# The last sums of y of the first pair of batches by accumulating GpSimd transfers, and other weights of two engines in the planner

## The chip, the cores and the metric

The kernel runs on one core of a Trainium2 chip. The metric is the device time of one execution in microseconds (us). The kernel before took 1038.81 us in the median of three runs (1038.71 to 1040.23).

The engines of the core are named as the profile names them: PE multiplies matrices (PEld loads its weights), DVE is VectorE, ACT is ScalarE, POOL is GpSimd, and SP only issues transfers (SPq is its queue). Each engine works through its own instructions strictly in order, so an instruction that waits holds up everything behind it on that engine.

## The reference

The input is four batches of attention with twelve heads, followed by two feed-forward blocks. Without the set-up it reads:

```python
# q, k, v: (4, 12, 448, 64)
scores = cap * tanh(q @ k.T / 8 / cap)          # cap = 30
attn = softmax(scores); x = attn @ v            # laid out as (1792, 768)
h = x @ w_in                                    # 768 -> 2048
g = h * cos(h)
y = g @ w_out                                   # 2048 -> 768
a = y @ w1; b = y @ w2                          # 768 -> 1024 each
out = (a * b @ w3) @ w_out2                     # 1024 -> 1024 -> 768
```

All inputs are 32-bit floats for the first part, and the weights come as 64-bit floats, which the kernel turns into 32-bit floats itself.

## The kernel before, in words

**Arithmetic.** A product of two 32-bit matrices is made of three passes on PE (lines 390, 391, 392): high half by high half, weight high by data low, weight low by data high. So each operand first has to be split into a high part (a cast, line 366 on ACT, 367 on DVE, 370 on POOL) and a low part (a subtraction, line 376 on DVE, 378 on POOL). Names that end in h and l are these parts (xh, xl, wih, wil, woh, wol). The 64-bit weights are converted by a scaling (lines 925 and 926), a masked copy (line 931, on POOL or, by the same line's other option, line 933 on DVE) and two bit operations on DVE (938 and 942).

**Stages.** Attention of all heads comes first, with the products of w3 and w_out2 (they don't depend on the data) mixed in. From about 160 us on, the first feed-forward block of the first pair of batches (b = 0 and 1) runs beside the attention of the second pair. Its work is cut into units: unit u is one group of 256 of the 2048 inner columns for one batch, and units of b = 0 and b = 1 take turns. A unit makes h with PE, its gate on ACT and DVE (the tile g with a high and a low part), and then y_part (line 1126 and on) multiplies g by two slices of w_out into six banks of PSUM, one for each m from 0 to 5. Each y_part is six passes of 448 columns, three for each of the unit's two blocks of 128 inner columns. The first group's y is copied into the tile y; every later group's is added to it (TENSOR_TENSOR y<-bank,y). After the last unit of a batch SP writes the six slices of y to DRAM (y_d). The second pair of batches uses seven products instead of eight in a two-by-two scheme of blocks (h_step); for it x_lefts loads the stored x, makes sums and differences of the blocks and splits them all, and h_rights does so for the weights. A product of this kind has three steps k, each of three passes. While h_step of the first pair of columns runs, PE also does the twelve y_parts of the last two units of b = 0 and 1. Later early_lefts loads y_d of b = 0 and 1 and prepares the second block, which fills the rest of the time.

**What sets the order.** Nothing is issued in the order of the source. Each piece of work is given to a planner (class Plan) with a due time, a list of engines that could do it with the planner's cost on each, and what it reads and writes. schedule goes through time, takes the ready pieces by due time, and gives each to the engine with the smallest sum of its waiting time and its cost. The cost is multiplied by a weight wACT, wDVE or wPOOL while the due time is below tw; before, all three weights were 1. A helper named port tells which pieces need the port that DVE and POOL share; by it every piece on POOL does. The planner's result is one fixed list of instructions for each engine. The same file holds a second, general program for large values of cap, which isn't executed with cap = 30.

Of the kernel before, what the change touches and what calls it, by code (L numbers as in the profile page):

```python
# [15 lines left out]
ALU = mybir.AluOpType  # L16
# [4 lines left out]
B, H, S, D = 4, 12, 448, 64  # L21
# [10 lines left out]
BH = B // 2  # L32
# [105 lines left out]
class Plan:  # L138
# [57 lines left out]
    def schedule(self):  # L196
# [10 lines left out]
        free = dict(PE=1.0, ACT=2.0, DVE=3.4, POOL=1.5, SP=1.2, port=0.0)  # L207

        def port(x):
            return x[0] == "POOL" or len(x) > 3  # L210

        free[None] = 0.0
        table, order, t, line = "exp", [], 0.0, 0.0
# [94 lines left out]
    wlead=3.1,  # L308


    wACT=1.0, wDVE=1.0, wPOOL=1.0, tw=396.0, back=1.13,
    nq=1, nqh=2, nph=2, npl=2,
    nraw=3, nx=2, w3bufs=2, w2bufs=6,
)
# [1 line left out]
    tw=432.21,  # L316
# [24 lines left out]
def program(  # L341
# [12 lines left out]
    general=False,  # L354
):
    nc = tc.nc
    PE, ACT, DVE, POOL, SP = nc.tensor, nc.scalar, nc.vector, nc.gpsimd, nc.sync
    G = dict(PAR, **GENERAL) if general else PAR
    plan = Plan()
# [4 lines left out]
    def copy(due, dst, src, n, on, psum=False):  # L364
        opts = {
            "A": ("ACT", (0.051 if psum else 0.094) + n / 1200, lambda: ACT.copy(dst(), src())),  # L366
            "D": ("DVE", 0.068 + n / (960 if psum else 1920), lambda: DVE.tensor_copy(dst(), src()))  # L367
            + (() if psum else (True,)),
            "P": ("POOL", 0.16 + n / 1200,
                  lambda: POOL.tensor_scalar(dst(), src(), 1.0, 0.0, op0=ALU.mult, op1=ALU.add)),  # L370
        }
        plan.op(due, [opts[e] for e in on], r=[src], w=[dst])
# [12 lines left out]
    def dma(due, dst, src, r=(), w=(), kb=115, write=False):  # L385
        plan.op(due, [("SP", 0.66, lambda: SP.dma_start(dst(), src()))], r=r, w=w,
                kb=kb)

    def mm3(out, wh, wl, xh, xl, first, last, on=False):
        PE.matmul(out, wh, xh, start=first, stop=False, skip_group_check=on)  # L390
        PE.matmul(out, wh, xl, start=False, stop=False, skip_group_check=on)  # L391
        PE.matmul(out, wl, xh, start=False, stop=last, skip_group_check=on)  # L392
# [60 lines left out]
    psum = pools["psum"].pool  # L453
# [24 lines left out]
    y_d = Scratch("dram", [B, KD, P, S], "y_d")  # L478
# [538 lines left out]
    def pair_due(n):  # L1017
        d = G["pd"]
        return unit_due(2 * NP) + (n - 0.26 * (n > 1)) * d
# [36 lines left out]
    def moe1(raw_r, x_r):  # L1056
# [14 lines left out]
        of = {b: [u for u, x in enumerate(units) if x[1] == b] for b in range(B)}  # L1071
# [58 lines left out]
        def y_part(u, m, due):  # L1130
            g, b = units[u]
            gh, gl = g_t[u]
            if u == of[b][0] and m == 0:
                yacc[b] = y_r.new()
            acc = hy_r.ref()
            ws = [w_t["o", g, c] for c in range(2)]

            def f():
                for c in range(2):
                    mm3(acc()[:, :S], ws[c][0]()[:, m * P:(m + 1) * P], ws[c][1]()[:, m * P:(m + 1) * P],  # L1140
                        gh()[:, c, :], gl()[:, c, :], c == 0, c == 1)

            plan.op(due, [("PE", 6 * MM, f)], r=[gh, gl, *ws[0], *ws[1]], w=[acc])
            ya = yacc[b].at(m, lambda t: t[:, m, :])
            if u == of[b][0]:
                copy(due + 1, ya, acc[:, :S], S, "AD", psum=True)
            else:
                tt(due + 1, ya, acc[:, :S], ya, S, ALU.add, psum=True)
            if u == of[b][-1]:
                z = y_d.at((b, m), lambda d: d[b, m])  # L1150
                dma(due + 3, z, ya, r=[ya], w=[z], kb=230, write=True)

# [137 lines left out]
        for u, (g, b) in enumerate(units[:2 * NP]):  # L1290
# [4 lines left out]
            for c in range(2):  # L1295
                wi = w_t["i", g, c]
                hp = hy_r.ref()
                for kp in range(3):
                    due = u0 + (c * 3 + kp) * pu / 6
# [3 lines left out]
                            r=[*wi, *(z.at(k) for k in ks for z in (xh[b], xl[b]))], w=[hp])  # L1303
# [14 lines left out]
        for n in range(NP):  # L1318
            u, u0, u1 = 2 * NP + 2 * n, pair_due(n), pair_due(n + 1)
# [415 lines left out]
```

## Time and profile before

| | |
|---|---|
| median of 3 runs | 1038.81 us |
| the profiled execution | 1039.48 us |
| its span (first to last instruction) | 1037.7 us |
| PE busy | 1012.4 us (98% of the span) |
| DVE busy | 934.6 us (90%) |
| ACT busy | 576.2 us (56%) |
| POOL busy | 254.8 us (25%) |
| transfers | 174.36 MB, mean 168 GB/s |

How to read it: 1.78 us of the profiled execution lie outside its span. Busy time is a union over the instructions of an engine; on PE and DVE an instruction starts before the one ahead has ended, so the sum of durations is larger than the busy time. The granted clock of PE was full for the whole span but for one short stretch near 495 us and the time after the last matmul.

### The profile page before, as it was taken

What the parts mean: (1) busy time and instruction counts of PE and PEld (TensorE: products, weight loads), DVE (VectorE), ACT (ScalarE), POOL (GpSimd) and SP (SyncE); (2) the same over time, 40 slices, a digit from 0 to 9 for tenths busy, and PEclk for the clock granted to TensorE, in tenths of its full rate; (3) what the DMA queues carried; (4) which work ended last, traced back from release to release, by engine and by line L of the source; (5) the groups of instructions that cost most, each with busy time, mean ns of one, the idle gap of its engine ahead of it and who ended that gap; (6) DMA issues with size and microseconds to landing.
All of it is one profiled execution on the core that took longest, in us unless ns stands there. A gap on an engine that the chain in (4) does not pass through costs nothing.

```text
span 1037.7 us, 15441 instructions
## 1 busy us (share of the span) xinstructions
PE 1012.4 (98%) x5524; PEld 864.6 (83%) x5524; DVE 934.6 (90%) x1418; ACT 576.2 (56%) x799; POOL 254.8 (25%) x203
## 2 busy tenths in 40 slices
PE   7999999989999999999999999999999999999997
PEld 2577777757788887798899999999898999999996
DVE  5999999999999999999999889999899889777982
ACT  6778787888777777725464433543334346222440
POOL 3453220222344321225303223211122100111110
PEclk9999999999999999999999999999999999999999
DMA  8776896867665655653545321319455556433442
GB/s 273 199 199 188 224 252 175 229 186 206 210 178 189 195 155 165 190 173 112 203 130 180 109 62 46 122 49 302 146 195 185 166 154 228 149 123 121 138 134 83
DMA packets 86648, 174.36 MB, mean 168 GB/s; under 512 B 19874, under 2 KB 59682, under 8 KB 86562
## 3 DMA queue, kind: packets, MB, share of 16 engines
q1 hardware_dynamic: 86562, 173.28, 54.4%
q8 instruction: 45, 0.74, 0.3%
q14 instruction: 41, 0.34, 0.1%
HBM read 131.30 MB, written 41.77 MB: 167 GB/s over the span
## 4 chain that ended last, share of the span: by engine, by line
PE 78%; DVE 11%; DMA 5%; issue 3%; ACT 1%; POOL 1%; SPq 1%; DVEq 0%; POOLq 0%; ACTq 0%
PE bank L390 23%; PE bank L392 23%; PE bank L391 22%; PE bank L702 4%; PE double L659 2%; PE double L658 2%; PE bank L707 1%; DMA rawc<-in_w_out 1%; DMA rawc<-in_w_in 1%; DMA kr<-in_k 1%; DVE stl L938 1%; DVE p L376 1%; DVE xl L376 1%; PE double L648 1%; DMA rs<-zs 1%
## 5 line engine op out<-in xcount | busy, mean ns | idle before, releaser
L390 PE MATMUL bank<-g,woh 128*128 128x448 f32 x384 | 140.6, 366 | 3.8 <-DVE zs L367 2.8
L392 PE MATMUL bank<-g,wol 128*128 128x448 f32 x384 | 139.1, 362 | 0.0
L391 PE MATMUL bank<-g,woh 128*128 128x448 f32 x384 | 138.8, 361 | 0.0
L673 ACT ACTIVATE double<-double,ts 112x896 f32<-112x896 f32 x96 | 93.8, 982 | 29.9 <-PE double L659 22.6
L376 DVE TENSOR_TENSOR y<-bank,y 128x448 f32<-128x448 f32 x168 | 101.5, 616 | 9.1 <-PE bank L392 8.8
L673 ACT ACTIVATE p<-double,pac 112x896 f32<-112x896 f32 x96 | 96.5, 1014 | 3.1 <-PE bank L707 1.8
L366 ACT COPY hs<-bank 128x448 f32<-128x448 f32 x74 | 39.4, 532 | 105.7 <-PE bank L392 105.6
L390 PE MATMUL bank<-xh,wih 128*128 128x448 f32 x264 | 96.6, 366 | 1.3 <-ACT xh L366 1.3
L391 PE MATMUL bank<-xl,wih 128*128 128x448 f32 x264 | 96.0, 364 | 1.2 <-POOL xl L378 1.2
L392 PE MATMUL bank<-xh,wil 128*128 128x448 f32 x264 | 96.5, 366 | 0.7 <-POOL wil L378 0.7
L390 PEld LDWEIGHTS bank<-g,woh 128*128 128x128 f32 x384 | 72.2, 188 | 15.2 <-DVE zs L367 3.2
L702 PE MATMUL bank<-p,v 112*32 112x448 f32 x768 | 77.6, 542 | 1.0 <-ACT w L1102 1.0
L392 PEld LDWEIGHTS bank<-g,wol 128*128 128x128 f32 x384 | 72.2, 188 | 5.2
L391 PEld LDWEIGHTS bank<-g,woh 128*128 128x128 f32 x384 | 72.1, 188 | 4.8
L931 POOL TENSOR_SCALAR wx<-rawc 128x768 f32<-128x768 f32 x29 | 39.8, 1371 | 94.7 <-ACT rawc L925 72.6
L376 DVE TENSOR_TENSOR p<-p 112x448 f32<-112x448 f32 x79 | 58.3, 738 | 2.4 <-ACT p L673 2.0
L702 PEld LDWEIGHTS bank<-p,v 112*32 112x32 f32 x768 | 22.3, 109 | 45.0 <-issue 41.0
L658 PE MATMUL double<-qh,ks 128*112 128x448 f32 x160 | 58.7, 367 | 0.0
L659 PE MATMUL double<-ql,ks 128*112 128x448 f32 x160 | 58.3, 365 | 0.0
L390 PEld LDWEIGHTS bank<-xh,wih 128*128 128x128 f32 x264 | 49.8, 189 | 8.3 <-issue 2.9
L391 PEld LDWEIGHTS bank<-xl,wih 128*128 128x128 f32 x264 | 49.8, 189 | 5.0 <-POOL xl L378 1.5
L392 PEld LDWEIGHTS bank<-xh,wil 128*128 128x128 f32 x264 | 49.9, 189 | 4.5 <-POOL wil L378 1.1
(356 smaller groups left out, 2786.0 us busy)
## 6 DMA issues: line engine op xcount, KB each, us to landing
rawc<-in_w_out SPq DMA_DIRECT2D x16, 768.0 KB, 5.4
stl<-w_d SPq DMA_DIRECT2D x32, 384.0 KB, 3.9
rawc<-in_w_in SPq DMA_DIRECT2D x13, 768.0 KB, 5.5
qr<-in_q SPq DMA_DIRECT2D x41, 224.0 KB, 4.3
kr<-in_k SPq DMA_DIRECT2D x41, 224.0 KB, 4.6
raw<-in_w3T SPq DMA_DIRECT2D x16, 512.0 KB, 5.3
raw<-in_w_out SPq DMA_DIRECT2D x8, 768.0 KB, 6.2
wo_d<-wx SPq DMA_DIRECT2D x16, 384.0 KB, 5.6
```

Source lines behind the costliest of these rows:

```text
L366: "A": ("ACT", (0.051 if psum else 0.094) + n / 1200, lambda: ACT.copy(dst(), src())),
L376: "D": ("DVE", 0.068 + n / 960, lambda: DVE.tensor_tensor(dst(), a(), b(), op=op))
L390: PE.matmul(out, wh, xh, start=first, stop=False, skip_group_check=on)
L391: PE.matmul(out, wh, xl, start=False, stop=False, skip_group_check=on)
L392: PE.matmul(out, wl, xh, start=False, stop=last, skip_group_check=on)
L648: PE.matmul(s()[:CP, j, :S], w()[r, k * CP:(k + 1) * CP], q()[r], start=True, stop=True)
L658: PE.matmul(o, w, qh(), start=True, stop=False)
L659: PE.matmul(o, w, ql(), start=False, stop=True)
L673: lambda f=f, x=x, o=o: ACT.activation(o(), s(), f, scale=x[:CP]))],
L702: PE.matmul(pv()[q * Q:(q + 1) * Q, :S], w()[:, j, c, d:d + Q], piece(j, c), **flags)
L707: PE.matmul(z()[q:q + Q, :S], one(), piece(j, 2 * c), start=True, stop=True)
L931: lambda: POOL.tensor_scalar(x(), h_().bitcast(F32), 0.0, 1.0, op0=ALU.mult, op1=ALU.mult)),
```

## The change

It has three parts. In y_part, the last unit of b = 0 and of b = 1 no longer adds to the tile y. The tile is written to y_d after the unit before the last one; the last unit's result is copied over the tile (by ACT or DVE), and a transfer issued by POOL adds the tile to y_d in DRAM. There are twelve of these transfers, two batches by six slices of 128 partitions x 448 numbers. In the planner's numbers, wDVE goes from 1.0 to 1.5 and wPOOL from 1.0 to 2.0, and tw from 396 to 2000, so the weights hold for every piece. The helper port lets a piece on POOL say that it needs no shared port, which the new transfers do.

```diff
         def port(x):
-            return x[0] == "POOL" or len(x) > 3
+            return x[3] if len(x) > 3 else x[0] == "POOL"
...
-    wACT=1.0, wDVE=1.0, wPOOL=1.0, tw=396.0, back=1.13,
+    wACT=1.0, wDVE=1.5, wPOOL=2.0, tw=2000.0, back=1.13,
...
             if u == of[b][0]:
                 copy(due + 1, ya, acc[:, :S], S, "AD", psum=True)
+            elif b < BH and u == of[b][-1] and not general:
+                copy(due + 1, ya, acc[:, :S], S, "AD", psum=True)
+                z = y_d.at((b, m), lambda d: d[b, m])
+                plan.op(due + 2, [("POOL", 1.0, lambda: POOL.dma_start(z(), ya(), accum_op=ALU.add), False)],
+                        r=[ya], w=[z], kb=400)
             else:
                 tt(due + 1, ya, acc[:, :S], ya, S, ALU.add, psum=True)
-            if u == of[b][-1]:
+            if u == of[b][-1 if general or b >= BH else -2]:
                 z = y_d.at((b, m), lambda d: d[b, m])
                 dma(due + 3, z, ya, r=[ya], w=[z], kb=230, write=True)
```

Over the executed program POOL issues 45 compute instructions and 12 transfers where it issued 203 instructions; DVE has 1482 where it had 1418, and ACT 867 where it had 773 (its table loads, 26 in both, not counted).

The order of PE where the products of the second pair of batches begin. g_1796 and g_1793 are the gate of the last unit of b = 0 (before and now), g_2001 and g_2014 that of b = 1; xh_479 with xl_497 (now xh_480 with xl_495) is the left operand of the first two products, and wih_1450 (now wih_1470) the right operand of the first pair of columns. Before:

```order
L392 MATMUL bank_3732<-g_1796,wol_2202 128x448
L390 MATMUL bank_76<-xh_479,wih_1450 128x448
L391 MATMUL bank_76<-xl_497,wih_1450 128x448
L392 MATMUL bank_76<-xh_479,wil_1468 128x448
L390 MATMUL bank_76<-xh_479,wih_1450 128x448
L391 MATMUL bank_76<-xl_497,wih_1450 128x448
L392 MATMUL bank_76<-xh_479,wil_1468 128x448
L390 MATMUL bank_76<-xh_479,wih_1450 128x448
L391 MATMUL bank_76<-xl_497,wih_1450 128x448
L392 MATMUL bank_76<-xh_479,wil_1468 128x448
L390 MATMUL bank_3733<-xh_479,wih_1397 128x448
L391 MATMUL bank_3733<-xl_497,wih_1397 128x448
```

The same place now:

```order
L392 MATMUL bank_3732<-g_1793,wol_2201 128x448
L390 MATMUL bank_75<-g_2014,woh_2118 128x448
L391 MATMUL bank_75<-g_2014,woh_2118 128x448
L392 MATMUL bank_75<-g_2014,wol_2164 128x448
L390 MATMUL bank_75<-g_2014,woh_2187 128x448
L391 MATMUL bank_75<-g_2014,woh_2187 128x448
L392 MATMUL bank_75<-g_2014,wol_2201 128x448
L390 MATMUL bank_3733<-xh_480,wih_1470 128x448
L391 MATMUL bank_3733<-xl_495,wih_1470 128x448
L392 MATMUL bank_3733<-xh_480,wil_1482 128x448
```

One y_part of b = 1 now stands between the sixth y_part of b = 0 and the first product. What followed the first product before was a product of the next pair of columns (weights wih_1397 and wil_1408); now it is the second product of the same pair.

The order of DVE up to the low half of the gate of the last unit of b = 1, before. The rows y<-bank are the sums of y of b = 0, rawx and qx are blocks of x:

```order
L376 TENSOR_TENSOR rawx_4013<-rawx_4013 128x448
L376 TENSOR_TENSOR xS1l_4133<-rawx_4013,xS1h_4096 128x448
L376 TENSOR_TENSOR rawx_4013<-rawx_4013 128x448
L376 TENSOR_TENSOR xS3l_4181<-qx_4004,xS3h_4058 128x448
L376 TENSOR_TENSOR xS2l_4157<-rawx_4013,xS2h_4108 128x448
L376 TENSOR_TENSOR y_1978<-bank_78,y_1978 128x448
L376 TENSOR_TENSOR y_1978<-bank_77,y_1978 128x448
L376 TENSOR_TENSOR y_1978<-bank_75,y_1978 128x448
L376 TENSOR_TENSOR y_1978<-bank_3732,y_1978 128x448
L376 TENSOR_TENSOR xl_1345<-rawx_4013,xh_1337 128x448
L376 TENSOR_TENSOR g_2001<-w_1916,g_2001 128x896
L376 TENSOR_TENSOR xl_497<-rawx_3981,xh_479 128x448
```

The same place now:

```order
L376 TENSOR_TENSOR y_2091<-bank_3733,y_2091 128x448
L376 TENSOR_TENSOR xl_1348<-rawx_3983,xh_1332 128x448
L376 TENSOR_TENSOR qx_4052<-rawx_4022 128x448
L1115 SCALAR_TENSOR_TENSOR w_1917<-kk_1688,w_1917 128x448
L376 TENSOR_TENSOR rawx_4022<-rawx_4022,qx_4054 128x448
L376 TENSOR_TENSOR xl_1348<-qx_4054,xh_1332 128x448
L376 TENSOR_TENSOR rawx_4022<-rawx_4022 128x448
L367 CAST xS3h_4060<-qx_4052 128x448
L376 TENSOR_TENSOR w_1917<-w_1917,hs_1909 128x896
L376 TENSOR_TENSOR xS1l_4145<-rawx_4022,xS1h_4104 128x448
L376 TENSOR_TENSOR rawx_4022<-rawx_4022 128x448
L376 TENSOR_TENSOR xS2l_4155<-rawx_4022,xS2h_4143 128x448
```

The next rows now are xS3l_4101, the low half of the gate g_2014, xl_1348 and xl_495 (the low half for the first product's last step). After the last sum of y of the unit before (y_2091) no sum of y stands in this stretch any more.

The order of POOL in the same part of the program, before:

```order
L378 TENSOR_TENSOR stx_4002<-stx_4039,stx_4029 128x384
L370 TENSOR_SCALAR xh_1337<-rawx_3981 128x448
L370 TENSOR_SCALAR wih_1397<-stx_4029 128x768
L378 TENSOR_TENSOR xl_497<-rawx_4013,xh_479 128x448
L378 TENSOR_TENSOR xl_497<-rawx_3981,xh_479 128x448
L378 TENSOR_TENSOR wil_1408<-stx_4029,wih_1397 128x768
L378 TENSOR_TENSOR stx_4015<-stx_4039,stx_4002 128x384
```

and now, from the last conversions of weights of the first block on:

```order
L931 TENSOR_SCALAR wx_1827<-rawc_1708 128x768
L931 TENSOR_SCALAR wx_1773<-rawc_1698 128x768 x2
L1150 DMA y_d<-y_1987 128x448 x6
L1150 DMA y_d<-y_2091 128x448 x6
L931 TENSOR_SCALAR stx_4058<-rawx_3983 128x768
L931 TENSOR_SCALAR stx_4017<-rawx_4022 128x768
```

POOL takes no part in x_lefts and h_rights any more; the twelve transfers are all that it does between the first block's weights and the second block's.

## Rows read from the trace of the kernel before

**Rows 1.** The page, part 1: busy us, share of the span, instructions
```profile
PE 1012.4 (98%) x5524; PEld 864.6 (83%) x5524; DVE 934.6 (90%) x1418; ACT 576.2 (56%) x799; POOL 254.8 (25%) x203
```

**Rows 2.** Busy us by stretch: from:to, length, engines (instructions), PEclk, DMA share, GB/s
```profile
30.00:465.00 435.00, 428.27 (x2607) 333.96 (x2596) 415.70 (x619) 326.52 (x405) 133.55 (x99) 1.00 0.67 194
213.50:216.40 2.90, 0.09 (x2) 0.06 (x1) 2.87 (x4) 2.87 (x4) 1.45 (x1) 1.00 1.01 298
490.00:494.70 4.70, 1.55 (x5) 0.86 (x5) 4.70 (x9) 2.17 (x5) 3.39 (x2) 1.00 0.30 110
494.70:498.20 3.50, 3.40 (x9) 3.06 (x10) 3.50 (x3) 0.00 (x0) 3.21 (x3) 0.51 0.79 253
552.00:1031.00 479.00, 477.22 (x2377) 444.69 (x2375) 413.89 (x641) 179.52 (x288) 85.01 (x74) 1.00 0.43 142
```

**Rows 3.** Waits of PE: line, who released it; us, times, longest
```profile
PE double L648 <- ACT p L673: 3.3, 3, 2.0
PE bank L390 <- DVE zs L367: 2.8, 1, 2.8
```

**Rows 4.** Timeline of PE, 487 to 500 us: start, us, instruction, idle before
```profile
489.59 0.36 PE L392 MATMUL bank<-xh,wil 128*128 128x448 f32 x1
491.29 0.47 PE L390 MATMUL bank<-xh,wih 128*128 128x448 f32 x1 [1.34 <-ACT xh L366]
492.99 0.48 PE L391 MATMUL bank<-xl,wih 128*128 128x448 f32 x1 [1.23 <-POOL xl L378]
...
494.80 0.74 PE L392 MATMUL bank<-xh,wil 128*128 128x448 f32 x1 [0.73 <-POOL wil L378]
...
498.23 0.36 PE L392 MATMUL bank<-g,wol 128*128 128x448 f32 x1
```

**Rows 5.** Timeline of POOL, 490 to 520 us
```profile
491.31 1.63 POOL L378 TENSOR_TENSOR xl<-rawx,xh 128x448 fp32r<-128x448 f32 x1 [7.80 <-ACT xh L366]
492.90 1.85 POOL L378 TENSOR_TENSOR wil<-stx,wih 128x768 fp32r<-128x768 f32 x1
...
513.68 2.85 POOL L378 TENSOR_TENSOR stx<-stx,stx 128x384 f32<-128x384 f32 x1 [15.77 <-DMA stx<-wi_d]
```

**Rows 6.** Timeline of DVE, 482 to 498 us
```profile
482.42 0.61 DVE L376 TENSOR_TENSOR y<-bank,y 128x448 f32<-128x448 f32 x1
...
488.19 1.08 DVE L376 TENSOR_TENSOR w<-w,hs 128x896 f32<-128x896 f32 x1
489.19 0.61 DVE L376 TENSOR_TENSOR rawx<-rawx 128x448 f32<-128x448 f32 x1
489.72 0.62 DVE L376 TENSOR_TENSOR xS1l<-rawx,xS1h 128x448 fp32r<-128x448 f32 x1
...
495.15 1.89 DVE L376 TENSOR_TENSOR g<-w,g 128x896 fp32r<-128x896 f32 x1
```

**Rows 7.** The page, part 5: groups of instructions: busy, mean ns, idle before
```profile
L376 DVE TENSOR_TENSOR y<-bank,y 128x448 f32<-128x448 f32 x168 | 101.5, 616 | 9.1 <-PE bank L392 8.8
...
L366 ACT COPY hs<-bank 128x448 f32<-128x448 f32 x74 | 39.4, 532 | 105.7 <-PE bank L392 105.6
...
L376 DVE TENSOR_TENSOR p<-p 112x448 f32<-112x448 f32 x79 | 58.3, 738 | 2.4 <-ACT p L673 2.0
```

**Rows 8.** Groups of DVE by shape, the same columns
```profile
L376 DVE TENSOR_TENSOR x<-xs,rb 128x448 f32<-128x448 f32 x24 | 18.4, 767 | 1.4 <-DMA rb<-rs_d 1.4
...
L942 DVE SCALAR_TENSOR_TENSOR x<-raw,x 128x512 uint32<-128x512 uint32 x16 | 11.2, 701 | 0.1
...
L938 DVE SCALAR_TENSOR_TENSOR stx<-rawx,stx 128x768 uint32<-128x768 uint32 x4 | 3.8, 950 | 0.0
```

**Rows 9.** Transfers: issuing queue, count, KB each, median us to landing
```profile
y_d<-y SPq DMA_DIRECT2D x24, 224.0 KB, 2.7
```

**Rows 10.** Timeline of SP's queue, 455 to 560 us
```profile
485.44 8.98 SPq L386 DMA_DIRECT2D y_d<-y  x6
...
508.11 0.32 SPq L386 DMA_DIRECT2D stx<-wi_d  x1
```

## The prediction

> **What bounds the kernel now.** I read the page's part 1 first. PE is busy for 98% of the span and DVE for 90%; ACT has nearly half of its time free and POOL three quarters [rows 1]. So PE sets the end wherever it is fed, and an edit is worth only what it takes away from PE's waits or adds to them. Busy time by stretch shows where such waits can be. From 552 us to 1031 us PE is busy for 477.22 of 479 us and DVE has 65 us free: nothing is to be had there, and a new wait would only cost. From 30 to 465 us PE is short of 6.7 us of 435, and DVE of 19.3 us, so DVE is close to being the bound [rows 2]. The waits of PE name two large ones in the first half, 3.3 us for exponentials at the start and 2.8 us for a DVE copy near 214 us [rows 3]. The third place is where the products of the second pair of batches begin. PE's timeline shows three waits inside twelve passes: for a cast on ACT (1.34 us), for the low half of x on POOL (1.23) and for the low half of a weight on POOL (0.73), and then passes at half speed [rows 4]. The granted clock in the 3.5 us after the waits was 0.51 of full, which is the lower level, 1.2 GHz, after a stretch of 4.7 us in which PE was busy for 1.55 us; in the single wait near 214 us, with PE busy for 0.09 of 2.9 us, it stayed at 1.00, 2.4 GHz [rows 2]. From 489.59 to 498.23 us there are 15 starts, which at the 0.2 us between undisturbed passes take 3.0 us; they took 8.64. This place costs 5.6 us.
>
> **The change part by part.** The sum is made against the profiled execution, 1039.48 us (1037.7 of span and 1.78 around it). The median shown is 0.67 us lower, and the change in time is carried over to it.
>
> *The start of the second pair.* Two things change here. POOL drops out: the two operations that PE waited for took 1.63 and 1.85 us on it [rows 5], and DVE does the same shapes now. And DVE loses the sums of y of b = 0 that stood between its pieces (four in a row before the gate's low half). The order of PE puts a y_part of b = 1 ahead of the first product, and the product of the next pair of columns, which waited for the weight, is gone from this place. So the new y_part's second pass, which takes the low half of the gate, decides. I count it on DVE from the last sum of y of the unit before, which began at 482.42 us [rows 6] and follows PE in both kernels. From that sum to the gate's low half stand, by the new order, eleven operations of 448 columns (one of them is the sum itself, and one, xS3l, comes just after the rows shown), one cast and one product of 896 columns. Starts of 448 columns are 0.53 us apart (489.19 and 489.72), the 896 columns take 1.00 (488.19 to 489.19) [rows 6], and the cast some 0.4, an estimate from half the 0.2 to 0.6 that copies and sums of this size take [rows 7]. That is 5.8 + 1.0 + 0.4 = 7.2 us, so the low half starts at 489.6 and is done at 490.7, since its 896 columns take as long as the product's, 1.08. PE reaches the y_part at 489.59 less five starts, 488.6, does one pass, and waits until 490.7: 1.9 us. The y_part then takes 1.0 us and the first two steps of the product 1.2, so PE asks for the last low half of x at 493.1; two operations after the gate it is there at 491.8. So 1.9 us stand against 5.6: a gain of 3.7. The bounds: 5.6 if DVE is ahead and nothing waits, and nothing if DVE is 2 us later and the pause brings the slow clock again. With the 2.9 us wait near 214 us as the nearest row, I take the clock as staying up.
>
> *The sums of y.* Twelve additions on DVE of 616 ns become twelve copies, all on ACT by the order, of 532 ns [rows 7]. They stand between 484 and 518 us, where ACT was busy for 2.17 of 4.7 us and DVE for all of it [rows 2]. ACT's free time hides the copies; DVE's 7.4 us are part of the gain just counted. The earlier stores of y move into SP's queue between the loads of x: SP now waits there for the sums of y, where it waited 8.98 us later [rows 10]. The loads of the last blocks come behind the six stores of b = 1 and so at 483 us at the earliest, about where the last of them stood. No charge, and 2 us if they come late.
>
> *The twelve transfers.* The trace has no transfer issued by POOL. The nearest row is SP's plain store of the same tile, 2.7 us to landing [rows 9]. An addition in DRAM also has to read what is there, so I bound it by 2.7 and three times that, 8.1, and take 5. POOL has nothing else to do at that time. SP's queue loads y_d back behind them, and behind those loads stand the weights of a later pair of columns, issued at 508.11 [rows 10], for which POOL ended a wait at 513.68 [rows 5]. The last transfer that this load waits for can start at about 503, with its y_part, and lands at 508. Cost: nothing, as far as 5 us hold.
>
> *The weights in the planner.* Over the program 158 compute instructions leave POOL, 64 more stand on DVE and 94 more on ACT. Up to 465 us DVE gets 40 masked copies (13 of 512 columns, 27 of 768), 15 more low halves and differences, and gives up 17 casts and copies. The trace has no masked copy on DVE; the bit operations on the same tiles take 701 and 950 ns [rows 8], which I take, as they read the same strided words. That is 9.1 + 25.7 for the masked copies, some 12 for the 15 at about 0.8, less 10.5 for the 17 at 0.616: 36 us, and 33 of busy time, since starts overlap by 0.08. DVE had 19.3 us free in that stretch. But DVE also waits beside POOL: sums of 448 columns take 616 ns from PSUM and 738 or 767 between two tiles of SBUF [rows 7, 8], though the starts without POOL show 0.61 for both kinds [rows 6]. These two rows alone are 79 x 0.122 + 24 x 0.151 = 13.3 us, and all SBUF operations of DVE have such a share; p and x are 103 of the some 500 of them there, so an estimate by count is 40 to 60. POOL keeps 33 of 107 compute instructions, so seven tenths of it go, 28 to 42. Added 33, removed about as much: I take 0. The ends are 33 - 19.3 = 14 us lost, if nothing is removed, and the 6.7 us that PE waits there, gained.
>
> In the second half ACT takes most casts and has 300 us free; nothing is charged. The sum is 1039.48 - 3.7 = 1035.8 for the execution, and 1035.1 for the median.
>
> One rule speaks against the transfers. The Trainium skill's page "SBUF — State Buffer" (section "A bandwidth-pool intuition that's wrong") says that a transfer issued by GpSimd which takes about 620 ns alone takes about 3100 beside a DVE copy, because DVE holds the port that the descriptors are written through. No run here shows it yet. By it each transfer would be some 2.5 us later, an estimate from that page, and the sum would stay as it is, since 5 us were allowed; it raises the chance of the third rival.
>
> **The rivals.**
>
> 1. *The place near 490 us costs as much as before.* For it: DVE had no idle time there, and its own low half of the gate began only at 495.15 [rows 6], so if DVE runs 2 us late, the wait is 3.9 us with the slow clock. Against it: four sums fewer and no waiting beside POOL. Then the time is 1038.8.
>
> 2. *DVE becomes the bound before 465 us.* This is the side of slower. It decides once less than 14 of the 33 us come back through POOL's absence. For it: DVE is within 19.3 us of full [rows 2]. Against: the waits in rows 7 and 8. With none coming back it is 1035.1 + 14 = 1049; with half of what is needed, 1042.
>
> 3. *The additions in DRAM land late.* If they take over 8 us each or are worked off one by one, SP's queue stands still before the weights of the later columns, and PE waits for these us for us. Twelve in a row at 5 us are 60 us from 490 on, against loads that begin at 503: some 10 to 30 us, 1045 to 1065. Against it: the transfers' engines are busy for 0.30 to 0.79 of the time there [rows 2].
>
> 4. *The other early waits go too.* The 3.3 and 2.8 us [rows 3] end at ACT and DVE, which work with less POOL beside them: 1029.
>
> **How the numbers follow.** The forecast has 0.44, rival 1 0.22, rival 2 0.18, rival 3 0.07 and rival 4 0.09. A measurement of this kernel tells about 0.2% from no change, 2.1 us. Of the forecast, whose own range is 1032 to 1037.5, a small part falls within that; with rival 4 faster has 0.50. Same has 0.24, from rival 1 and the edges of the forecast and of rival 2; slower has 0.26. The range is 1029.5 to 1044: it takes in rival 4 and the milder half of rival 2 and leaves out the full price of rivals 2 and 3.
>
> **What would show it.** PE's timeline between 488 and 497 us (in the kernel after, where the gate's last y_part comes first): one wait of about 2 us for a DVE low half of g, at full clock, says the first step is right; waits of over 3.5 us or a granted clock of 0.5 say rival 1. DVE's groups should show p<-p near 0.62 to 0.65 us instead of 0.738, and POOL's busy time near 60 us. PE's busy share from 30 to 465 us should stay within 3 us of 428; a drop says rival 2. The loads from y_d and the weights behind them in SP's queue should be issued no later than 510 us; a wait of PE between 515 and 560 us says rival 3. The forecast is wrong if PE loses more than 3 us at any new place.

## The result and the profile after

The changed kernel takes 1029.72 us in the median of four runs (1029.49 to 1030.38); the kernel before, run beside it, 1039.07. The ratio is 0.9901, with a 95% interval of 0.9886 to 0.9916. So it is faster by some 9 us, where 3.7 were forecast. The direction was right and the size more than twice the forecast; the time lies just inside the lower end of the range.

The profiled executions differ by as much: a span of 1028.1 us against 1037.7. PE does the same 5524 passes in both, so each pass number can be looked up in both traces (their order differs in places ahead of pass 1600 and behind pass 2850). Pass 2850 lies just ahead of the place where the second pair of batches begins, and by pass 3000 that place is over. Pass 2850 starts at 486.6 us before and at 482.0 now; the 150 passes behind it, which take 30.0 us at 0.2 us each, took 35.7 and now 31.4; from pass 3000 to the last one it is 508.7 and 508.0. So 4.6 us came from the part ahead of the place, 4.3 from the place itself and 0.7 from what follows, 9.6 in all. This split is that of one execution of each kernel: the profiled one of the kernel before had a mean granted clock of 0.997, the 62 executions of it beside the experiments 0.994 in the median (0.992 to 0.998), so most of them ran longer at half clock than the one shown.

Where the early part was gained can be read more closely. From pass 1600 to pass 2850 both kernels do the same passes in the same order (before, then now; the columns as in [rows 2]):

```profile
267.43:486.59 219.16, 219.16 (x1252) 181.82 (x1250) 209.46 (x301) 146.33 (x183) 76.92 (x56) 1.00 0.57 178
262.81:481.97 219.16, 219.16 (x1251) 181.83 (x1250) 211.19 (x328) 157.37 (x197) 23.49 (x20) 1.00 0.59 186
```

PE is fed throughout in both. So the 4.6 us all came ahead of pass 1600, which starts at 267.4 us before and at 262.8 now.

Part 1 of the page of the changed kernel, for [rows 1] (busy us, share of the span, instructions):

```profile
PE 1008.3 (98%) x5524; PEld 864.1 (84%) x5524; DVE 913.0 (89%) x1482; ACT 637.1 (62%) x893; POOL 61.0 (6%) x57
```

DVE has 64 instructions more and is busy for 21.6 us less. That is the first line to be surprised at, and what the prediction had not expected. Only 6.1 of these us lie ahead of pass 2850; 5.4 lie at the place and 10.1 behind it, where PE gained only 0.7.

Busy time by stretch in the changed kernel, the columns as in [rows 2]. The first stretch ends 4 us earlier than that of before, as its work does:

```profile
30.00:461.00 431.00, 427.86 (x2610) 334.95 (x2603) 411.48 (x657) 349.49 (x441) 35.56 (x28) 1.00 0.67 197
484.30:485.50 1.20, 0.08 (x2) 0.04 (x1) 1.20 (x3) 1.20 (x4) 0.00 (x0) 1.00 1.13 211
485.50:492.00 6.50, 6.50 (x33) 6.10 (x34) 6.50 (x13) 3.92 (x8) 3.46 (x4) 1.00 1.05 168
552.00:1022.00 470.00, 467.67 (x2332) 436.60 (x2330) 395.03 (x644) 204.08 (x324) 9.73 (x7) 1.00 0.42 138
```

PE is short of 3.1 us in the first stretch, where it was short of 6.7. POOL works for 36 us there instead of 134. DVE is as close to full as it was (19.5 us free of 431, 19.3 of 435 before), and the two waits of PE that are left in this stretch, 1.0 and 2.1 us, are both for DVE.

The waits of PE (line, who released it: us, times, longest), for [rows 3]:

```profile
PE bank L390 <- DVE zs L367: 2.1, 1, 2.1
PE double L648 <- ACT p L673: 2.0, 1, 2.0
PE bank L390 <- ACT hs L366: 1.2, 1, 1.2
PE bank L391 <- DVE g L376: 1.1, 1, 1.1
PE bank L391 <- DVE w2l L376: 1.0, 1, 1.0
```

The two large early ones are shorter, not gone. Of the smaller ones, 0.3 to 1.0 us each up to 261 us, one is left (w2l, near 35 us). Part of that is chance: e1 below has the order of before up to the place, and its profile lacks the waits near 101, 208 and 260 us. No wait names POOL any more.

The timeline of PE at the start of the second pair, for [rows 4]:

```profile
483.97 0.37 PE L390 MATMUL bank<-g,woh 128*128 128x448 f32 x1
485.46 0.47 PE L391 MATMUL bank<-g,woh 128*128 128x448 f32 x1 [1.12 <-DVE g L376]
485.76 0.37 PE L392 MATMUL bank<-g,wol 128*128 128x448 f32 x1
```

One wait, for the instruction that the prediction named, and no slow passes behind it: the granted clock is 1.00 (2.4 GHz) in the wait and in the 6.5 us after it.

The timeline of DVE up to that low half, for [rows 6]:

```profile
477.12 0.62 DVE L376 TENSOR_TENSOR y<-bank,y 128x448 f32<-128x448 f32 x1
...
481.17 1.09 DVE L376 TENSOR_TENSOR w<-w,hs 128x896 f32<-128x896 f32 x1
...
483.78 0.62 DVE L376 TENSOR_TENSOR xS3l<-qx,xS3h 128x448 fp32r<-128x448 f32 x1
484.31 1.09 DVE L376 TENSOR_TENSOR g<-w,g 128x896 fp32r<-128x896 f32 x1
```

From the last sum of y to the low half it is 7.19 us.

Groups of instructions, for [rows 7, 8], with the masked copies that DVE did not have before (line engine op out<-in, shapes, count | busy us, mean ns | idle before):

```profile
L376 DVE TENSOR_TENSOR p<-p 112x448 f32<-112x448 f32 x80 | 52.1, 651 | 3.2 <-ACT p L673 3.1
L376 DVE TENSOR_TENSOR x<-xs,rb 128x448 f32<-128x448 f32 x24 | 14.8, 616 | 0.0
L376 DVE TENSOR_TENSOR y<-bank,y 128x448 f32<-128x448 f32 x156 | 95.7, 618 | 7.7 <-PE bank L392 7.1
L376 DVE TENSOR_TENSOR wol<-wx,woh 128x768 fp32r<-128x768 f32 x32 | 29.7, 951 | 0.3 <-ACT woh L366 0.3
L933 DVE TENSOR_SCALAR wx<-rawc 128x768 f32<-128x768 f32 x16 | 8.9, 554 | 0.1
L933 DVE TENSOR_SCALAR x<-raw 128x512 f32<-128x512 f32 x13 | 5.5, 424 | 4.4 <-POOL raw L926 3.8 <-ACT raw L925 0.4
```

The two groups between tiles of SBUF went from 738 and 767 ns to 651 and 616; the sums that read a bank of PSUM stayed (616 and 618). The masked copies take 424 and 554 ns.

The twelve transfers and SP's queue behind them, for [rows 9, 10] (the first row: issuing queue, count, KB each, median us to landing; the others: start, time in SP's queue):

```profile
y_d<-y POOLq DMA_DIRECT2D x12, 224.0 KB, 5.5
```

```profile
485.42 9.39 SPq L386 DMA_DIRECT2D rawx<-y_d  x3
495.50 0.32 SPq L386 DMA_DIRECT2D stx<-wi_d  x1
...
504.90 0.32 SPq L386 DMA_DIRECT2D qx<-y_d  x1
```

SP does stand behind the additions (9.39 us over three loads from y_d), but the weights behind it start at 495.50, and PE has no wait of over 0.2 us between 486 and 739 us.

### The profile page after: what moved, and what is told of

It reads as the page before. It is cut to its first block, busy times and chain, and to the rows that moved or that the text cites. A ratio compares the mean times of both kernels' runs of the same rounds, so it can differ in the third digit from the quotient of the medians.

```text
span 1028.1 us, 15309 instructions
## 1 busy us (share of the span) xinstructions
PE 1008.3 (98%) x5524; PEld 864.1 (84%) x5524; DVE 913.0 (89%) x1482; ACT 637.1 (62%) x893; POOL 61.0 (6%) x57
## 4 chain that ended last, share of the span: by engine, by line
PE 92%; DVE 3%; ACT 2%; issue 1%; DMA 1%; SPq 0%; ACTq 0%; DVEq 0%
PE bank L390 26%; PE bank L392 25%; PE bank L391 25%; PE bank L702 7%; PE double L658 3%; PE double L659 3%; PE bank L707 2%; PE double L648 1%; ACT double L673 1%; ACT p L673 1%; DVE xl L376 1%; DMA qr<-in_k 0%; DVE y L376 0%; DVE rawx L376 0%; SPq L386 0%
## 5 line engine op out<-in xcount | busy, mean ns | idle before, releaser
L376 DVE TENSOR_TENSOR y<-bank,y 128x448 f32<-128x448 f32 x156 | 95.7, 618 | 7.7 <-PE bank L392 7.1
L366 ACT COPY hs<-bank 128x448 f32<-128x448 f32 x83 | 44.4, 535 | 88.4 <-PE bank L392 88.3
L376 DVE TENSOR_TENSOR p<-p 112x448 f32<-112x448 f32 x80 | 52.1, 651 | 3.2 <-ACT p L673 3.1
L366 ACT COPY w<-bank 128x448 f32<-128x448 f32 x26 | 13.9, 534 | 56.4 <-PE bank L392 56.4
```

Of the source, the lines that this page charges most:

```text
L376: "D": ("DVE", 0.068 + n / 960, lambda: DVE.tensor_tensor(dst(), a(), b(), op=op))
```

## The experiments

Each kernel is the changed one or the one before with one edit. The ratios are to the kernel before, run on the same chip beside it (its medians there were 1039.4 to 1040.1 us).

For all of them the same three stretches were read off the traces, and DVE's load ahead of pass 2850. The load is split in two: "alone" is the sum of what its instructions take undisturbed, for which each shape's tenth percentile over all the kernels stands; "extra" is what they took beyond that.

| kernel | median us | pass 2850 at | 150 passes there | rest | DVE alone + extra | POOL's operations |
|---|---|---|---|---|---|---|
| before | 1039.07 | 486.6 | 35.7 | 508.7 | 452.8 + 47.0 | 159.6 |
| changed | 1029.72 | 482.0 | 31.4 | 508.0 | 479.3 + 16.5 | 40.7 |
| e1 | 1040.05 | 484.4 | 37.6 | 508.7 | 453.3 + 46.8 | 151.1 |
| e2 | 1036.60 | 482.6 | 37.6 | 508.1 | 477.9 + 15.3 | 43.8 |
| e3 | 1039.27 | 485.2 | 38.3 | 508.0 | 486.1 + 11.3 | 36.1 |
| e4 | 1046.41 | 490.7 | 40.0 | 506.7 | 423.9 + 64.7 | 188.2 |
| e5 | 1057.73 | 496.8 | 38.7 | 515.8 | 479.3 + 27.8 | 306.4 |
| e6 | 1037.14 | 484.9 | 34.7 | 509.3 | 479.3 + 14.8 | 100.9 |
| e7 | 1035.61 | 482.2 | 36.2 | 508.8 | 483.0 + 6.3 | 4.9 |
| e8 | 1034.45 | 489.4 | 31.3 | 508.2 | 459.4 + 28.0 | 84.8 |
| e9 | 1029.95 | 482.0 | 31.4 | 508.1 | 479.3 + 15.6 | 42.3 |
| e10 | 1038.72 | 481.1 | 38.6 | 508.0 | 477.9 + 17.2 | 43.3 |
| e11 | 1030.92 | 481.4 | 30.8 | 508.1 | 479.3 + 15.1 | 40.0 |
| e12 | 1029.64 | 480.6 | 31.1 | 508.1 | 475.1 + 16.2 | 46.4 |

The columns behind the median come from one profiled execution of each kernel. Those of e5 and e8 were 3.2 and 3.0 us above the median of their runs, those of e10 and e11 were 2.3 and 1.9 below. Two executions with the same order of DVE up to about 465 us (before and e1) differ by 2.2 us at pass 2850; differences of that size in that column are not read as effects.

**e1: the transfers alone.**

```diff
-    wACT=1.0, wDVE=1.5, wPOOL=2.0, tw=2000.0, back=1.13,
+    wACT=1.0, wDVE=1.0, wPOOL=1.0, tw=396.0, back=1.13,
```

> The twelve accumulating transfers alone, with the planner's weights of before (all 1, up to 396); POOL keeps its 200 compute instructions. Theory A (most of the gain is POOL's absence from the port that it shares with DVE, and from the pieces that PE waits for; the transfers matter little): POOL is still a releaser at the start of the second pair and the early waits near 34, 58, 101, 207 and 213 us stay; 1036 to 1039.5, a ratio to before of 0.997 to 1.000. Theory B (the four sums of y that leave DVE ahead of the gate's low half make the gain, as the prediction's first term had it): the waits near 490 us go from 5.6 to under 2.5 us and the time is 1034 to 1036.

Ratio 1.0014 (1.0002 to 1.0027), 1040.05 us: no gain. Theory B falls in this form. Theory A's range is missed by 0.6 us, and POOL did not release PE at the place as it had it. PE's order is the new one, with the y_part ahead of the first product, but PE waits there 2.4 us for the gate's high half on ACT and 2.1 us for its low half on DVE, and then runs at half clock. Two DVE operations of 448 columns at 474 and 476 us took 1.43 us each, where 0.61 is usual.

**e2: the weights alone.**

The edit is to the kernel before:

```diff
-    wACT=1.0, wDVE=1.0, wPOOL=1.0, tw=396.0, back=1.13,
+    wACT=1.0, wDVE=1.5, wPOOL=2.0, tw=2000.0, back=1.13,
```

> The planner's weights alone (VectorE 1.5, GpSimd 2.0, for every piece), the last sums of y on DVE as before, no accumulating transfer. Theory A: POOL busy near 60 us, DVE's p<-p near 0.65 us, the early waits as small as with the whole change (3.1 us of gaps between 30 and 465 us where before had 6.7), and near 490 us no POOL wait and no slow clock; 1029 to 1032. Theory B: without the transfers the place near 490 us still loses 4 to 5 us, 1033 to 1036.

Ratio 0.9971 (0.9960 to 0.9983), 1036.60 us: a gain of 3.5 us. In the profiles pass 2850 comes 4.0 us sooner, and the place takes 1.9 of it back: it costs 7.6 us instead of 5.7. So neither half of the change helps the place by itself, and the gains of e1 and e2 (none, and 3.5 us) do not add up to 9. That each half makes the place worse is seen in one profile of each kernel, and the kernel before ran at half clock for longer in most executions than in its profile. Theory A is right for the early part and wrong for the place; theory B's range is missed by 0.6 us.

**e3 and e4: one weight at a time.**

```diff
-    wACT=1.0, wDVE=1.5, wPOOL=2.0, tw=2000.0, back=1.13,
+    wACT=1.0, wDVE=1.0, wPOOL=2.0, tw=2000.0, back=1.13,   (e3)
+    wACT=1.0, wDVE=1.5, wPOOL=1.0, tw=2000.0, back=1.13,   (e4)
```

> The whole change but VectorE's weight at 1.0 (GpSimd 2.0): DVE gets 1522 instructions, 40 more than with the whole change and 104 more than before, POOL 45. Theory A (POOL's absence pays for the DVE work that it brings): DVE's p<-p near 0.65 us, 1029 to 1033. Rival C (what counts is how many instructions DVE has; VectorE's weight is what keeps it from being the bound): PE loses 5 us or more beside DVE before 465 us, 1035 to 1042.

> The whole change but GpSimd's weight at 1.0 (VectorE 1.5): POOL gets 256 instructions, 53 more than before, DVE 1318, 100 fewer. Theory A: DVE's operations between two tiles of SBUF are as slow as before or slower (p<-p 0.74 us or more), POOL's pieces come late, and the time is that of before or worse, 1038 to 1045. Rival C: with 100 instructions fewer DVE is no longer near its bound and the early waits go, 1028 to 1032.

e3 has the ratio 0.9995 (0.9986 to 1.0004), e4 1.0068 (1.0053 to 1.0082). e4 is the clearest against rival C: DVE has 100 instructions fewer than before and 29 us less work of its own, but 65 us of extra beside a POOL that works for 188 us, and PE comes 4 us later; theory A's upper edge is passed by 1.4 us. e3 is neither theory: its 1039.27 us lie in rival C's range, but PE is short of only 3.95 us from 30 to 465 us where C named 5 or more. It has little extra (11 us), but 33 us more work than before, and its place is among the worst. Both weights were needed in these kernels: GpSimd's takes the extra away, and with VectorE's DVE has 40 instructions fewer and ACT 28 more.

**e5 and e6: POOL made busy again, and the control.** About 120 places were meant; the traces have 124, evenly spread over the plan's order:

```diff
...
+            tick = ticks[n // step % 2]
+            ACT.copy(tick, quarter)
+            z = tick.to_broadcast([P, 80])                     (e5)
+            for _ in range(5):
+                POOL.tensor_tensor(idle, z, z, op=ALU.add)
+            POOL.tensor_tensor(idle[:, 0:1], tick, tick, op=ALU.add)   (e6)
```

> The changed kernel with POOL busy again: at 120 places, evenly spread over the order, ACT copies one column to a small tile and POOL makes five sums of 128 x 80 from it (an estimated 0.33 us each, 195 us in all, as much as the change took off POOL). No result of them is used; the order of the other instructions of DVE, ACT, PE and SP is that of the changed kernel. Theory A (POOL at work makes DVE's operations between two tiles of SBUF longer, and DVE's lateness is what PE waits for): p<-p goes from 0.651 towards 0.74 us, the low half of the gate at the start of the second pair comes 2 to 5 us late and the slow clock follows; 1034 to 1041. Rival D (the gain is in the new order itself and in which engine has which piece, not in the port): p<-p may move, the time stays at 1029 to 1032.

> The control for the kernel with POOL busy again: the same 120 small copies on ACT, and one sum of one column on POOL behind each. Both theories: as the changed kernel, 1029 to 1032, p<-p near 0.65 us. If it is slower than 1032, the copies on ACT are a part of what the loaded kernel shows and its difference is to be taken from here.

e5 has the ratio 1.0174 (1.0156 to 1.0193), 1057.73 us, far above the 1041 that theory A allowed; e6 has 0.9965 (0.9950 to 0.9980), 1037.14 us. The control was not neutral: it lost 7 us against the changed kernel, so only the difference between the two counts. It is large: 20.6 us by the medians. In the profiles it is 23.1, 11.9 of them ahead of pass 2850, where DVE's extra rises by 13.0 us with the same instructions in the same order, 4.0 at the place and 6.5 behind it. One group in e5, in e6 and in e7, which has hardly any work on POOL, and the sums from PSUM in e5:

```profile
L376 DVE TENSOR_TENSOR p<-p 112x448 f32<-112x448 f32 x80 | 56.9, 711 | 1.7 <-ACT p L675 1.6
L376 DVE TENSOR_TENSOR y<-bank,y 128x448 f32<-128x448 f32 x156 | 94.7, 613 | 4.5 <-PE bank L392 4.4
```

```profile
L376 DVE TENSOR_TENSOR p<-p 112x448 f32<-112x448 f32 x80 | 50.7, 633 | 3.3 <-ACT p L675 3.1
```

```profile
L376 DVE TENSOR_TENSOR p<-p 112x448 f32<-112x448 f32 x80 | 49.4, 619 | 5.4 <-ACT p L673 5.2
```

That a busy POOL lengthens DVE's operations between tiles of SBUF is shown. That PE pays for it one to one is not: ahead of pass 2850 DVE also waited 19.9 us for POOL's own pieces, which now stood between the sums (10.9 in e6, 6.3 in the changed kernel), and the profile of e5 has two stretches of 3.4 us at half clock ahead of 35 us. Rival D's time did not come, but that the new order has a part in the early gain is not excluded.

At the place theory A's mechanism did not come in e5: the low half of the gate kept PE waiting for 1.48 us, at full clock. Most of what was lost there, and part of what the control lost there, came by the transfers. In e6 a sum of one column on POOL lasted for 12.58 us, and the twelve transfers stand behind it. The rows are POOL's, then ACT's, then PE's:

```profile
481.27 12.58 POOL L1703 TENSOR_TENSOR idle<-tick 128x1 f32<-128x1 f32 x1 [7.12 <-ACT tick L1702]
493.79 2.89 POOL L1152 DMA_DIRECT2D y_d<-y  x3
...
502.76 0.56 ACT L366 CAST yA11h<-rawx 128x448 fp32r<-128x448 f32 x1 [3.06 <-DMA rawx<-y_d]
503.24 0.53 ACT L366 COPY hs<-bank 128x448 f32<-128x448 f32 x1
...
503.81 0.47 PE L390 MATMUL bank<-xS3h,ht 128*128 128x448 f32 x1 [1.55 <-ACT hs L366]
```

The first transfer was issued at 493.79 us, in the changed kernel at 479.04. The load of y_d behind the transfers came late for ACT, and PE waited for ACT's next copy. In e5 five sums took 15.27 us at the same place, the first transfer was issued at 508.61, and PE waited 3.14 us for the same copy, with 6.8 us at half clock. This is the mechanism of the prediction's rival 3, with a cause that it did not name: work of POOL ahead of the transfers.

**e7: no conversions on POOL.** The changed kernel with `wPOOL=100.0`.

> The changed kernel with GpSimd's weight at 100 instead of 2: its last 35 conversions go to DVE (1504 where the changed kernel has 1482) and ACT (880 for 867); POOL only memsets and issues the 12 transfers. Theory A: 39 us less at work on POOL is worth a little more on DVE, which also no longer waits 3.8 us for POOL's scalings; the time is 1027 to 1030 as long as 22 more DVE instructions do not make the gate later. If DVE's lag at the start of the second pair is what counts, more instructions on DVE ahead of it cost: 1032 to 1038 with the slow clock there.

Ratio 0.9965 (0.9952 to 0.9978), 1035.61 us, the second of the two cases. Ahead of pass 2850 it is like the changed kernel (482.2 and 482.0), and the extra is nearly gone, but the place costs 6.2 us: waits of 2.0 us for the gate on ACT and 2.1 on DVE, and the half clock. Less contention did not help: DVE's work and extra together fell by 6.5 us ahead of pass 2850, PE came there no sooner, and the gate was late all the same. Why it was late here is not shown.

**e8: the masked copies left on POOL.**

```diff
             ("DVE", 0.07 + n / 960,
              lambda: DVE.tensor_scalar(x(), h_().bitcast(F32), 0.0, 1.0, op0=ALU.mult, op1=ALU.mult), True),
-        ], r=[r], w=[x])
+        ][:1], r=[r], w=[x])
```

> The changed kernel with the masked copies of the weights' conversion left on POOL by rule (it has no choice of DVE for them any more): POOL 109 instructions for 57, DVE 1433 for 1482. It takes from DVE some 20 us of work (13 x 0.42 and 27 x 0.55 us before 465 us) and gives POOL 52 instructions. Theory A: what DVE saves it pays back beside POOL, and the bit operations wait for POOL's copies; within 3 us of the changed kernel, 1028 to 1034. Rival C (DVE's instruction count decides): 1024 to 1028.

Ratio 0.9942 (0.9927 to 0.9958), 1034.45 us: rival C falls, and theory A's upper edge is passed by a little. DVE has 20 us less work of its own and 11.5 more extra, which alone would leave a gain; but it is idle for 12 us more ahead of pass 2850 (44.7 us for 32.4), and PE comes 7.4 us later. Near 214 us one wait of 2.8 us was followed by 6.8 us at half clock. That is the profile, 3.0 us above the median and with a mean granted clock of 0.993; the other five runs had 0.997 to 0.999, so the stretch at half clock is not typical of them.

**e9 and e10: one batch at a time.**

```diff
-            elif b < BH and u == of[b][-1] and not general:
+            elif b == 0 and u == of[b][-1] and not general:    (e9; b == 1 in e10)
```

(The earlier store is restricted to the same batch.)

> The changed kernel, but only the last unit of b = 0 is added by GpSimd transfers (six of them); the last unit of b = 1 is summed on DVE and stored by SP as before. DVE's order up to the low half of the gate at the start of the second pair is that of the changed kernel: no sum of y stands there. Theory L (what PE waits for there is how late DVE is with that low half, and the sums of b = 0 on DVE are what made it late): one wait of 1.1 us, full clock, as in the changed kernel; 1029 to 1031. Rival (the copies on ACT and the transfers of both batches matter, or the store's place in SP's queue): 1032 to 1037.

> The mirror image: only the last unit of b = 1 is added by GpSimd transfers, the six sums of b = 0 stand on DVE again, all ahead of the low half of the gate, as with the weights alone. Theory L: six sums at 0.53 us put the low half 3.2 us or more later; waits of 4 to 5 us for the gate on ACT and DVE and a stretch at half clock behind them, as with the weights alone; 1035 to 1038. Rival: as the changed kernel, 1029 to 1032.

e9 has the ratio 0.9904 (0.9890 to 0.9919), 1029.95 us; e10 0.9984 (0.9973 to 0.9995), 1038.72. That is as theory L had it (e10 is 0.7 us above its range), and it names the part of the transfers that counts: the six sums of b = 0 that they take off DVE. e9 differs from e2 only in what becomes of these six, and its ratio is lower by 0.0067, some 7 us. DVE in e10 at the place:

```profile
484.59 0.61 DVE L376 TENSOR_TENSOR xS3l<-qx,xS3h 128x448 fp32r<-128x448 f32 x1
485.12 2.21 DVE L376 TENSOR_TENSOR y<-bank,y 128x448 f32<-128x448 f32 x4
487.25 0.61 DVE L376 TENSOR_TENSOR xl<-rawx,xh 128x448 fp32r<-128x448 f32 x1
487.78 1.08 DVE L376 TENSOR_TENSOR g<-w,g 128x896 fp32r<-128x896 f32 x1
```

PE's waits in e10, and its clock (stretch, length, PE, PEld, DVE, ACT, POOL, PEclk, DMA share, GB/s):

```profile
PE bank L391 <- DVE g L376: 3.8, 1, 3.8
...
PE bank L390 <- ACT g L366: 1.4, 1, 1.4
```

```profile
483.20:489.00 5.80, 0.58 (x3) 0.27 (x2) 5.80 (x11) 2.37 (x5) 0.00 (x0) 0.93 0.76 277
489.00:495.00 6.00, 6.00 (x16) 5.37 (x17) 5.02 (x9) 1.91 (x5) 1.03 (x1) 0.50 0.51 116
```

Waits of 5.2 us in place of 1.1, and then 6.8 us at 1.2 GHz; in the 6.0 us of them shown PE does 16 passes, which is the time of 30 at 0.2 us. In all it is 38.6 us for the 150 passes against 31.4.

**e11 and e12: what is left.** The last gates due 3 us earlier; in e12 also the copies of zs and xs.

```diff
+            q = 3.0 if units[u][1] < BH and u == of[units[u][1]][-1] and not general else 0.0
-            tt(due + 6, w2, w2, h2, 2 * S, ALU.mult, "DP")
+            tt(due + 6 - q, w2, w2, h2, 2 * S, ALU.mult, "DP")
...
-            copy(at(g), x[n], y[:, :S], S, "AD", psum=True)
+            copy(at(g) - (0 if general else 3), x[n], y[:, :S], S, "AD", psum=True)   (e12)
```

> The changed kernel with the last gate of b = 0 and of b = 1 due 3 us earlier for the planner: on DVE one operation of 448 columns (xS3l) now stands behind the low half of the gate instead of ahead of it. Theory L: the wait of 1.1 us becomes 0.6, everything else stays: 1028.8 to 1030. If the place is not ruled by DVE's lateness: no change there.

> The same, and the copies out of the banks of the attention's sums (zs, xs) due 3 us earlier too, since PE's longest wait before 465 us in the changed kernel (2.1 us near 211 us) is for such a copy on DVE, behind an operation of 768 columns. That changes the planner's order of DVE from some 290 instructions on. If the wait goes and no other comes: 1027 to 1029. If the new order makes DVE late somewhere else, as other orders did: 1031 to 1038.

Ratios 0.9915 (0.9902 to 0.9928) and 0.9902 (0.9888 to 0.9916). In the profiles the waits did what was expected: in e11 the 1.1 us became 0.6, in e12 the 2.1 us near 211 became 0.7, and the spans are 1027.1 and 1026.5 us. Over the runs neither can be told from the changed kernel: the medians, 1030.92 and 1029.64 us, lie above the ranges that were expected. Here is e11:

```profile
PE bank L391 <- DVE g L376: 0.6, 1, 0.6
```

## Why the prediction was right in direction and wrong in size

**The start of the second pair: right.** The forecast was 5.6 us lost before, 1.9 after, a gain of 3.7; measured 5.7, 1.4 and 4.3. The count on DVE was exact: 7.2 us from the last sum to the low half were forecast, and 7.19 stand in the trace. The wait came out at 1.1 and not 1.9, because PE reached its pass 6.85 us after that sum and not 6.2. The bound for a DVE 2 us later, with the slow clock again, is what e2, e7 and e10 show. What the prediction did not see is that this gain needs both parts: with either alone the place costs 7.6 us in the profiles (e1, e2).

**The sums of y and the transfers: right.** The copies take 533 ns on ACT and hide there (e9 against the changed kernel: no difference for b = 1). The transfers landed in 5.5 us where 5 were taken; rival 3 did not come here (it did in e5 and e6). On the rule of the Trainium skill's page "SBUF — State Buffer" (section "A bandwidth-pool intuition that's wrong") that the prediction weighed: POOL was occupied for 0.86 to 0.88 us by most of them while DVE was busy throughout; whether part of the 5.5 us is a wait for the port no run here separates.

**The weights in the planner: the step that failed.** The prediction said: "Added 33, removed about as much: I take 0." The runs say that the early part came 4.6 us sooner in this pair of profiles; over the six kernels with the new order (changed, e2, e9 to e12) pass 2850 starts at 480.6 to 482.6, with the old weights (before, e1) at 486.6 and 484.4, 3.9 us on average. The two halves of the term: removed were 30.5 us of extra, inside the 28 to 42 that were forecast. (The count that this came from, 13.3 us for 103 of some 500 operations, gives 65 and not the 40 to 60 written; 47.0 were there, so the lower figure was the better one by luck.) Added were 26.5 us by the table's count ahead of pass 2850, where 36 were forecast. The masked copies account for more than that difference: priced at 701 and 950 ns after the bit operations, they take 424 and 554. The nearer rows were in the trace before: DVE's casts of 128x768, one tile in and one out like the masked copy, took 544 to 561 ns in six groups (others, longer in the mean, up to 743), while the bit operations read two tiles. One of those six, from the kernel before:

```profile
L367 DVE CAST xh<-stq 128x768 fp32r<-128x768 f32 x9 | 5.0, 552 | 0.0
```

With 13 and 27 masked copies at what they took it is 20.5 us instead of 34.8; the rest of what was added was priced some 5 us too low. By that the same working gives 33 - 14.3 = 18.7 us added against 28 to 42 removed, and so a gain bounded by the 6.7 us that PE waited there; 3.6 of these went. The Trainium skill's page "VectorE: DVE Perf Modes" (section "Mode 2×_2P — use both read ports for one tensor") has this: with one source in SBUF, DVE reads through both ports and makes two results a cycle, with two sources it cannot. The trace agrees: a 128x768 copy takes 554 ns and a difference of two such tiles (wol<-wx,woh) 951.

The stretch that the step summed over was wrong too: every one of those waits lies ahead of pass 1600, and there, by the same split of DVE's load, some 9 us were added and 17 removed. From pass 1600 to 2850 some 17 were added and 14 removed, and PE, which was fed throughout, paid nothing for it up to there. So the balance of the whole, 30.5 less 26.5, is no measure of the 4.6 us, near as it comes.

**The end.** 0.7 us came after pass 3000, where nothing was forecast. It goes with the planner's weights: with the old ones (before, e1) this stretch took 508.7 us, with the new ones (changed, e2, e9 to e12) 508.0 to 508.1.

**The rivals.** Rival 4 (1029 us, 0.09) is what came, though the two waits that it named shrank and did not go. Rival 1's mechanism, a late DVE and the slow clock, is what e2, e7 and e10 ran into. Rival 2 had the wrong sign: DVE's own work did grow by 26.5 us, and more than that came back. Most of the signs named ahead held: p<-p at 651 ns, POOL at 61 us, one wait on a DVE low half at full clock, the first seven loads from y_d by 505 us. An eighth and more weights came at 515 to 518 us, behind the 510 that were named, without a wait of PE. PE's busy time from 30 to 465 us, which was to stay within 3 us of 428, rose to 431.9.

Open are two things: how much of the early gain is the port and how much the order itself, since e5 and e6 put a load on POOL but not the one that was removed; and what the control e6 lost ahead of pass 2850 (2.9 us) and behind the place.

## What to carry to other kernels

Before pricing an instruction that moves to another engine, find rows with the same number of sources and the same memories, not the same tile: here one source against two was a factor of 1.7, and a term that was put at nothing was a gain. Draw the balance only over the stretch in which the bounding engine waits. Where DVE and POOL share a core that DVE bounds, POOL's work is not free: in the kernels where it did its ordinary work, each us of it ahead of pass 2850 went with some 0.3 to 0.4 us of extra on DVE (47.0 for 159.6 before, 16.5 for 40.7 after, 64.7 for 188.2 in e4; the many small sums of e5 cost less, 27.8 for 306.4). And parts of a change that meet at one wait can't be judged one by one: the transfers alone gave nothing, and on top of the weights they were worth some 7 us.

## What the runs showed of the hardware

The contention is not a slowing of all operations but a few that are held up. Of the 79 p<-p before, the median is 619 ns, as it is where POOL does next to nothing (e7); 16 took over 700 ns, the longest 2260, against 5 of 80 in the changed kernel and none in e7. Each of the 16 ended 0.48 or 0.49 us after an instruction of POOL that had ended inside it. Under the many small sums of e5 it was 37 of 80, with a median of 658. No sum from PSUM in the kernel before, the changed one or e7 took over 633. The Trainium skill's page "SBUF — State Buffer" (section "Who interferes with whom") says that DVE with two sources in SBUF and a POOL instruction that reads SBUF exclude each other for a whole instruction, and that DVE with at most one source in SBUF, outside its two-port modes, is spared; the trace agrees on both.

It holds POOL up as well. The sums of one column in e6 took 192 ns at the least, 515 in the median and up to 12.6 us; those of 80 columns in e5 318 at the least and 730 on average, where 330 were estimated. The longest in e6 began at 481.27 us; 22 operations of DVE between tiles of SBUF followed one on the other without a gap, and it ended at 493.85, just after DVE had begun a sum that reads a bank (493.72).

The half clock came in these stretches: in e10 it fell at the end of 5.8 us in which PE was busy for 0.58 (0.50 for 6.8 us then), in e7 after 4.8 us with 0.73 busy (0.50 for 3.4 us). In the 1.2 us of the changed kernel's wait, with 0.08 busy, it stayed at 1.00. In e10 it turned 4.1 us of additional waiting into 7.2.
